# Moving the order of work at three seams of an adaLN attention and gMLP kernel: the first products, the step from attention to the MLP, and the ends of the mixing blocks

## The chip, the core and the metric

The kernel runs on one core of one Trainium2 chip. A core has five engines that run beside each other and wait for one another through semaphores: TensorE (PE in the profile; its weight loads are listed apart as PEld), VectorE (DVE), ScalarE (ACT), GpSimd (POOL) and SyncE (SP), which here only issues DMAs. Each engine works through its own instructions in the order in which the program lists them, so an instruction that waits also holds everything behind it on its engine. Matmul results land in PSUM, which holds 8 banks of 128 x 512 floats here: a ring of seven shared by nearly everything, and one bank of its own.

The metric is the time of one execution on the device in microseconds (us); lower is better. Times of several executions are compared by their median.

## The reference

One block of a network on x of 2048 rows and 448 columns. A conditioning vector c gives six modulation vectors; attention with 16 heads of width 28 comes first, then a gated MLP that mixes along the sequence.

```python
mod = (_silu(c) @ w_mod).reshape(c.shape[0], 6, 1, -1)
sa, ca, ga, sb, cb, gb = ...
h = _layernorm(x) * (1 + ca) + sa
x = x + ga * _A_ref(h, A_wqkv, A_wo)
h = _layernorm(x) * (1 + cb) + sb
x = x + gb * _B_ref(h, B_w_in, B_w_sp, B_b_sp, B_w_out)

# _A_ref: q, k, v = h @ wqkv; p = softmax(q k^T * 28**-0.5); out = (p v) @ wo
# _B_ref: z = gelu(h @ w_in); z1, z2 = halves of z; z2 = layernorm(z2)
#         g = w_sp @ z2 + b_sp;  out = (z1 * g) @ w_out
```

The halves z1 and z2 have 896 columns each, and w_sp is 2048 x 2048.

## The kernel before, in words

Wherever an operand of a large product must keep its precision, it is split into a high part in the PE's fast float format and a low part that is the rest (`sub`, line 71), and the product is summed from three partial products. For an inner width of 448 this gives eleven matmuls per output tile, listed in `STEPS`; the last two of them, `STEPS_Z`, use only slot 6 of the left operand. A "V tile" below is one output of `v_tiles` (128 rows of V, eleven matmuls at line 256, copied out by DVE at line 258), and a "QK unit" is one call of `qk_unit` (128 channels of Q or K for 512 rows, eleven matmuls at line 265, copied and split by ACT and POOL, and written to scratch memory in DRAM by SP).

The stages, in the order of the program:

1. **The first products.** SP loads x in four groups of 512 rows (`load_x`), the modulation weights (`load_mod`, line 152) and wqkv (`load_w`, lines 165, 74, 75). DVE takes the layernorm statistics (`ln_stats`), sums the modulation products (`mod_acc`, lines 199 and 201), and normalises (`ln_norm`, line 238). `mod_col` turns the modulation sums into per-channel columns with PE (line 207) and DVE (line 211). `ln_transpose` transposes a group with PE (line 104) and applies the columns and the split with ACT, DVE and POOL (lines 111 to 122); its result is hT[g]. The loop over g (line 316) then does, for each group, its V tiles, the transposes of the next group, the statistics of the one after, and the QK units of channels 0 and 3 of the same group; before the first QK unit, the four parts of the QK weights are split by `weight_part` (line 353), the low parts by DVE and POOL in turn. All PSUM tiles of this stage come from the seven ring banks in turn, so the n-th tile waits until the reader of the tile seven before it is done.
2. **Attention.** Twenty further QK units are run with the first row-maximum products of head 0 between their matmuls (`m_first`, lines 535 to 548), in an order that needs only the first 1536 rows of q and k at first. Then a hand-written order (line 550) interleaves row-maximum products (line 388, reduced by DVE at line 393), score products (419), exponentials on ACT (423) and the products with V (434). Small per-head steps sit at numbered slots (`at`, `events`), DMAs among them. The result lands in OT, in `heapD`.
3. **The step to the MLP** (from line 666). The last head's sums are inverted (line 680), and its rows are scattered into OT by eight DMAs (line 471), half from SP and half from ACT. `win_load` loads the first half of w_in (lines 652, 74, 75) and `win_prep` splits it (lines 82 and 71). The output projection of 16 row tiles (`wo_mm`, line 599) runs for seven "held" tiles without `STEPS_Z`, then waits for `o_split(3, ...)`, the split of slot 6 (lines 486 to 488; the low parts by DVE and POOL in turn), and finishes them. `wo_add` adds x (line 619), `h2_stats` and `h2_norm` (line 638) do the second layernorm, `h2_group` the transposes, with all low parts on POOL.
4. **z1** (line 717) and **z2** (line 779), the two halves of the gelu product.
5. **Mixing.** For each of four blocks of 512 output rows (tb) and 16 key tiles (st) of w_sp, seven channel tiles (f) are summed into seven PSUM banks with three matmuls each (lines 825 to 827). A w_sp tile is loaded by SP (760), split by ACT (762) and DVE (71); there are two buffers for the raw tile and four for the split ones. The last `nj` key tiles of a block are run channel by channel, so that `gate` can start on a finished channel while PE sums the next: DVE adds and multiplies (lines 842 and 843), ACT and POOL split the result into uT. From the second block on, the output product of the block before (`y_part`, lines 865 to 871) is spread between the key tiles.

Most tiles of the large buffers are views into `heapD`, `heapA` and `heapB`. The lines that the change touches, and those that are named in the prediction:

Of the kernel before, what the change touches and what calls it, by code (L numbers as in the profile page):

```python
# [20 lines left out]
NG = 4  # L21
# [12 lines left out]
def tile_adaln_mha_gmlp(ctx, tc, x, wqkv, wo, w_in, w_spT, b_sp, w_out, cT, w_mod, out):  # L34
# [26 lines left out]
    heapD = dpool.tile([128, 24 * 896], F32R, name="heapD")  # L61
# [6 lines left out]
    wqk = hview(heapD, 14336, 8, 896)  # L68
# [8 lines left out]
    def weight_part(dst, i, raw, hi_eng, lo_eng, zero=True):  # L77

        n = raw.shape[-1]
        h = dst[:, i if i < 3 else 6, :n]  # L80
        if hi_eng is act:
            act.activation(h, raw, AF.Copy)
        else:
            hi_eng.tensor_copy(h, raw)
        if i < 3:
            sub(lo_eng, dst[:, 3 + i, :n], raw, h)
        else:
            sub(lo_eng, dst[0:64, 7, :n], raw[0:64], h[0:64])
            if zero:
                pool.memset(dst[64:128, 7, :n].bitcast(F32), 0.0)  # L90
# [6 lines left out]
    def ln_transpose(xns, full_pool, dsts, scol, bcol, engs, los=(pool,) * 4, mid=None, after=None):  # L97

        tps = []
        for c in range(4):  # L100
            tp = ring.tile([128, 512], F32, name="tp", tag="s")
# [46 lines left out]

    def load_mod(pair, eng):
# [23 lines left out]
    load_mod(0, sp)  # L173
# [3 lines left out]
    pool.memset(wqk[64:128, 7, :].bitcast(F32), 0.0)  # L177
# [8 lines left out]
    wu = ring.tile([128, 512], F32, name="wu", tag="s")  # L186
# [16 lines left out]
    def mod_col(*parts):  # L203
        pc = ring.tile([128, 512], F32, name="pc", tag="s")
        for i, (nm, acc, plus1) in enumerate(parts):
            for c, r, e in ((0, 0, 128), (1, 0, 128), (2, 0, 128), (3, 0, 64), (3, 64, 128)):
                pe.matmul(
                    pc[r:e, 4 * i + c : 4 * i + c + 1], acc[:, c * 128 : c * 128 + e - r], ones[:112, 0:1], start=True, stop=True
                )
        for i, (nm, acc, plus1) in enumerate(parts):  # L210
            dve.tensor_scalar(out=cols[nm], in0=pc[:, 4 * i : 4 * i + 4], scalar1=plus1, scalar2=None, op0=ALU.add)

    def mod_bc(nm, acc):
        pc = ring.tile([128, 512], F32, name="pc", tag="s")
# [18 lines left out]
    def ln_norm(g):  # L233
# [13 lines left out]
        for xn in res:  # L247
            pool.tensor_copy(xn[:, D:], xn[:, 384:D])
        return res

    def v_tiles(*kts):
        pvs = [ring.tile([128, 512], F32, name="pv", tag="s") for _ in kts]
# [7 lines left out]
    def qk_unit(m, g, mid=None):  # L260
        pq = ring.tile([128, 512], F32, name="pq", tag="s")
# [33 lines left out]
    def wv_rest(c):  # L295
        if c == 2:
            wv_hi(1)
# [4 lines left out]

    def mod_first():
        pe_fill(4)
        mod_col(("ca", accs[0][:, 1, :], 1.0), ("sa", accs[0][:, 0, :], 0.0))
# [6 lines left out]
    for i in range(4):  # L312
# [3 lines left out]
    for g in range(NG):  # L316
# [4 lines left out]
        if g == 3:  # L321
            early.close()
            stk = att.enter_context(tc.tile_pool(name="stk", bufs=1))
            kq = {}
            for i, (nm, pad) in enumerate((("k0", 64), ("q0", 0), ("q2", 16), ("k2", 0), ("q1", 8), ("k1", 8))):
                if pad:
                    stk.tile([128, pad], F32, name=f"pad{i}")
                kq[nm] = stk.tile([128, S], F32R, name=f"{nm[0]}st{nm[1]}")
            kst, qst = ([kq[f"{n}{i}"] for i in range(3)] for n in "kq")
# [11 lines left out]
            load_head(0, 0, 1536)  # L341
            for m in (0, 3):
                qk_unit(m, g)
            load_head(0, 1536, S)
# [6 lines left out]
        if g == 0:  # L351
            for i in range(4):
                weight_part(wqk, i, raws.pop(("qk", i)), act, (dve, pool)[i % 2], False)
# [5 lines left out]
        if g > 0:  # L359
            v_tiles(4 * g + 2)  # L360
        else:
            pool.memset(V[:, :, :, DH:32], 1.0)
        v_tiles(4 * g + 3)
        if g == 2:
            mod_bc("ga", accs[1][:, 0, :])
            mod_col(("sb", accs[1][:, 1, :], 0.0))
        if g < 3:
            for m in (0, 3):
                qk_unit(m, g)
        if g in (1, 2):  # L370
            for k in range(4):
                mod_acc(g, k)
    mod_col(("cb", accs[2][:, 0, :], 1.0))
# [11 lines left out]
    def m_mm(j, kb):  # L385
        h, t = divmod(j, NT)
        mt = ring.tile([128, 512], F32, name="mt", tag="s")
# [13 lines left out]
    def m_fin(h):  # L401
        mx = mxs.pop(h)
        tp = ring.tile([128, 512], F32, name="mtp", tag="s")
# [538 lines left out]
```

## Time and profile before

| | us |
|---|---|
| median of 3 executions | 1465.11 (1464.35 to 1467.84) |
| the profiled execution, its own time | 1466.46 |
| its span, first to last instruction | 1464.7 |

The profile is that of one execution. Its span is 1.8 us shorter than its own time; a duration from it is set against the span, and a forecast that is made as a difference is added to the median. "Busy" counts the time in which an engine executes; matmuls are pipelined, and their ends are modelled. A row of a timeline gives start, length, engine, line, operation, output and inputs, how many instructions are merged into it, and in brackets how long the engine had been idle before it and what ended that idle time. A row of the waits gives who waited for whom, the total in us, how many times, and the longest. A row of the windows gives, for one stretch of the span, its length, each engine's busy time with the number of instructions, the clock that was granted to TensorE (1.00 is full), the busy share of the DMA engines, and GB/s.

### The profile page before, as it was taken

What the parts mean: (1) busy time and instruction counts of PE and PEld (TensorE: products, weight loads), DVE (VectorE), ACT (ScalarE), POOL (GpSimd) and SP (SyncE); (2) the same over time, 40 slices, a digit from 0 to 9 for tenths busy, and PEclk for the clock granted to TensorE, in tenths of its full rate; (3) what the DMA queues carried; (4) which work ended last, traced back from release to release, by engine and by line L of the source; (5) the groups of instructions that cost most, each with busy time, mean ns of one, the idle gap of its engine ahead of it and who ended that gap; (6) DMA issues with size and microseconds to landing.
All of it is one profiled execution on the core that took longest, in us unless ns stands there. A gap on an engine that the chain in (4) does not pass through costs nothing.

```text
span 1464.7 us, 19637 instructions
## 1 busy us (share of the span) xinstructions
PE 1436.5 (98%) x7314; PEld 1015.3 (69%) x7314; DVE 884.6 (60%) x1440; ACT 733.1 (50%) x1390; POOL 302.0 (21%) x273
## 2 busy tenths in 40 slices
PE   5899999999999999999999999999999999999999
PEld 5787755555555555555555555888988888888887
DVE  6557888888888888888888832921552411413114
ACT  3523577677677767767776786442432211211111
POOL 6734200000002011001000021520763400302002
PEclk9999999999999999999999999999999999999999
DMA  7554401221022211221012004442002321313223
GB/s 220 146 163 151 145 9 46 52 49 43 15 52 53 53 39 40 53 51 41 21 47 52 11 19 139 151 149 101 8 14 99 119 77 67 113 64 106 84 69 107
DMA packets 56133, 111.24 MB, mean 76 GB/s; under 512 B 11901, under 2 KB 22781, under 8 KB 53517
## 3 DMA queue, kind: packets, MB, share of 16 engines
q1 hardware_dynamic: 55868, 109.76, 25.1%
q8 instruction: 57, 0.93, 0.3%
q10 hardware_dynamic: 168, 0.23, 0.1%
q14 instruction: 40, 0.32, 0.1%
HBM read 75.89 MB, written 29.48 MB: 72 GB/s over the span
## 4 chain that ended last, share of the span: by engine, by line
PE 92%; DVE 2%; POOL 2%; DMA 2%; issue 1%; ACT 0%; SPq 0%; ACTq 0%; DVEq 0%; POOLq 0%
PE st_ps L419 18%; PE mt L388 16%; PE o_ps L434 16%; PE acc L825 7%; PE acc L827 7%; PE acc L826 7%; PE z_ps L779 5%; PE z_ps L717 5%; PE pq L265 4%; PE y_ps L866 2%; PE y_ps L865 2%; PE y_ps L867 2%; PE pv L256 1%; PE tp L104 1%; POOL heapD L71 1%
## 5 line engine op out<-in xcount | busy, mean ns | idle before, releaser
L393 DVE TENSOR_REDUCE pm<-mt 128x1 f32<-128x512 f32 x1024 | 632.0, 681 | 121.8 <-PE mt L388 121.4
L423 ACT ACTIVATE P<-st_ps 128x512 f32<-128x512 f32 x1024 | 514.2, 618 | 154.3 <-PE st_ps L419 153.9
L419 PE MATMUL st_ps<-qst,kst 86*128 86x512 f32 x1024 | 409.8, 411 | 0.0
L388 PE MATMUL mt<-kst,qst 84*128 84x512 f32 x1024 | 406.6, 397 | 0.3 <-DVE pm L393 0.3
L419 PEld LDWEIGHTS st_ps<-qst,kst 86*128 86x128 f32 x1024 | 193.1, 189 | 144.8 <-issue 82.2
L434 PE MATMUL o_ps<-P,V 128*32 128x512 f32 x2048 | 247.5, 598 | 0.0
L388 PEld LDWEIGHTS mt<-kst,qst 84*128 84x128 f32 x1024 | 194.8, 190 | 38.3 <-DVE pm L393 0.7
L71 DVE TENSOR_TENSOR wsp_l<-raw_sp,wsp_h 128x512 fp32r<-128x512 f32 x64 | 53.7, 841 | 185.7 <-ACT wsp_h L762 185.7
L762 ACT ACTIVATE wsp_h<-raw_sp 128x512 fp32r<-128x512 f32 x64 | 40.3, 631 | 229.1 <-DMA raw_sp<-in_w_spT_dram 187.3
L434 PEld LDWEIGHTS o_ps<-P,V 128*32 128x32 f32 x2048 | 54.1, 109 | 123.5 <-issue 116.6
L71 POOL TENSOR_TENSOR heapD<-u,heapD 128x512 fp32r<-128x512 f32 x27 | 44.7, 1692 | 254.0 <-ACT heapD L844 170.2
L460 POOL TENSOR_TENSOR osb<-osb,rb 128x512 f32<-128x512 f32 x15 | 19.2, 1281 | 349.6 <-DMA rb<-r_scr 192.0
L265 PE MATMUL pq<-heapD 128*128 128x512 f32 x308 | 85.8, 396 | 2.9 <-DVE heapD L71 2.9
L825 PE MATMUL acc<-wsp_h,heapD 128*128 128x512 f32 x224 | 87.6, 391 | 0.6 <-DVE u L842 0.6
L827 PE MATMUL acc<-wsp_h,heapD 128*128 128x512 f32 x224 | 87.3, 390 | 0.0
L826 PE MATMUL acc<-wsp_l,heapD 128*128 128x512 f32 x224 | 87.2, 389 | 0.0
L265 PEld LDWEIGHTS pq<-heapD 128*128 128x128 f32 x308 | 58.0, 189 | 16.4 <-DVE heapD L71 3.4
L71 POOL TENSOR_TENSOR nl<-nf,nh 16x128 fp32r<-16x128 f32 x16 | 7.2, 453 | 285.5 <-issue 152.3
L267 ACT ACTIVATE qf<-pq 128x512 f32<-128x512 f32 x28 | 16.7, 597 | 70.1 <-PE pq L265 70.1
L870 DVE TENSOR_TENSOR x2t<-x2t,y_ps 128x448 f32<-128x448 f32 x12 | 7.5, 622 | 72.9 <-PE y_ps L867 72.9
L825 PEld LDWEIGHTS acc<-wsp_h,heapD 128*128 128x128 f32 x224 | 42.1, 188 | 9.7 <-DVE u L842 1.4
L71 POOL TENSOR_TENSOR ql<-qf,qh 128x512 fp32r<-128x512 f32 x28 | 36.4, 1304 | 59.7 <-ACT qh L269 47.2
(150 smaller groups left out, 1693.3 us busy)
## 6 DMA issues: line engine op xcount, KB each, us to landing
raw_sp<-in_w_spT_dram SPq DMA_DIRECT2D x64, 256.0 KB
kst<-qk_scr SPq DMA_DIRECT2D x45, 224.0 KB
qst<-qk_scr SPq DMA_DIRECT2D x45, 224.0 KB
qk_scr<-qh SPq DMA_DIRECT2D x28, 256.0 KB
qk_scr<-ql SPq DMA_DIRECT2D x28, 256.0 KB
z_scr<-z1t SPq DMA_DIRECT2D x28, 256.0 KB
z<-z_scr SPq DMA_DIRECT2D x28, 256.0 KB
wm<-in_w_mod_dram SPq DMA_DIRECT2D x12, 392.0 KB
```

Source lines behind the costliest of these rows:

```text
L71: eng.tensor_tensor(out=dst, in0=a, in1=hi.bitcast(F32), op=ALU.subtract)
L265: pe.matmul(pq, wqk[:, b, m * 128 : (m + 1) * 128], hT[g][:, a, :], start=j == 0, stop=j == NST - 1)
L388: pe.matmul(mt, qst[h % 3][0:84, t * 128 : (t + 1) * 128], kst[h % 3][0:84, kb * 512 : (kb + 1) * 512], start=True, stop=True)
L393: dve.tensor_reduce(out=pms[h][:, t, kb : kb + 1], in_=mt, axis=AX.X, op=ALU.max)
L419: pe.matmul(st, kst[h % 3][0:86, kt * 128 : (kt + 1) * 128], qst[h % 3][0:86, qb * 512 : (qb + 1) * 512], start=True, stop=True)
L423: act.activation(p, st, AF.Exp, scale=SCALE)
L434: pe.matmul(otile[h][32 * qb : 32 * qb + 32, :], V[:, kt, h, :], ptiles.pop((u, qb)), start=kt == 0, stop=kt == NT - 1)
L717: pe.matmul(ps_t, w1[:, b, f * 128 : (f + 1) * 128], h2T[g][:, a, :], start=j == 0, stop=j == NST - 1)
L779: pe.matmul(ps_t[:, :D], h2T[g][:, a, tt * 128 : (tt + 1) * 128], w2[:, b, hf * D : (hf + 1) * D], start=j == 0, stop=j == NST - 1)
L825: pe.matmul(acc[f], z2[st][:, 0, fs], hi, start=st == 0, stop=False)
L826: pe.matmul(acc[f], z2[st][:, 0, fs], lo, start=False, stop=False)
L827: pe.matmul(acc[f], z2[st][:, 1, fs], hi, start=False, stop=st == NT - 1)
```

## The change

It is one diff with edits in each of the stages.

- **First products.** The four DMAs of the first modulation weights are issued by ACT instead of SP. The 64-column copy at the end of a normalised tile moves from POOL to DVE. `mod_col` can do its columns in two halves; the first call does channels 0 and 2, then 1 and 3, and four warm-up matmuls ahead of it go. In the loop, the QK units of a group come one pass later: group 0 is done in pass 1, group 1 in pass 2, and groups 2 and 3 in pass 3, where all four stand ahead of the V tiles of group 3. Pass 0 does V tiles 0 to 2, then the transposes of group 1, then V tile 3, and then the split of the QK weights, with all four low parts on DVE. The first part of head 0 that is loaded back ends at row 1024 instead of 1536, and `first` is ordered to match. The buffers of q and k lose their padding and take another order.
- **w_in during the attention.** The last 4 x 896 columns of `heapD` become a buffer of their own, `heapF`; once the QK weights are done with, it holds the first half of w_in, which is loaded at slots 180 to 204 of the attention. `Halves` joins two buffers into one view.
- **The step to the MLP.** All four groups of x are loaded ahead of the last head's scatter; all four parts of w_in are split at the start of the stage. The scatter is dealt five to SP and three to ACT. Eight tiles are held instead of seven, the eighth in the bank beside the ring. The four low parts of `o_split(3, ...)` and the low parts of `h2_group` go to DVE, and the output tiles 12 to 15 are placed between the pieces of `h2_group`.
- **Mixing.** Every block ends with three key tiles by channel (before: two, and three in the last block). Ahead of the gates of a block, the split of one w_sp tile of the next block is listed instead of two; of the second one only the load is issued, and its split stands behind the gates.

```diff
-    heapD = dpool.tile([128, 24 * 896], F32R, name="heapD")
+    heapD = dpool.tile([128, 20 * 896], F32R, name="heapD")
+    heapF = dpool.tile([128, 4 * 896], F32R, name="heapF", tag="heapF")
...
+    wqk = Halves(4, hview(heapD, 14336, 4, 896), hview(heapF, 0, 4, 896))
...
-    load_mod(0, sp)
+    load_mod(0, act)
...
-            pool.tensor_copy(xn[:, D:], xn[:, 384:D])
+            dve.tensor_copy(xn[:, D:], xn[:, 384:D])
...
     def mod_first():
-        pe_fill(4)
-        mod_col(("ca", accs[0][:, 1, :], 1.0), ("sa", accs[0][:, 0, :], 0.0))
+        parts = ("ca", accs[0][:, 1, :], 1.0), ("sa", accs[0][:, 0, :], 0.0)
+        mod_col(parts, (0, 2))()
+        rest.append(mod_col(parts, (1, 3)))
         pe_fill(10)
...
-            load_head(0, 0, 1536)
-            for m in (0, 3):
-                qk_unit(m, g)
-            load_head(0, 1536, S)
+            load_head(0, 0, 1024)
+            for i in (2, 3):
+                for m in (0, 3):
+                    qk_unit(m, i)
+            load_head(0, 1024, S)
...
-        if g == 0:
-            for i in range(4):
-                weight_part(wqk, i, raws.pop(("qk", i)), act, (dve, pool)[i % 2], False)
         if g + 1 < NG:
             ln_transpose(xns, e1, hT[g + 1], cols["ca"], cols["sa"], (act,) * 4)
         if g + 2 < NG:
             ln_stats(g + 2)
             xns = ln_norm(g + 2)
-        if g > 0:
+        if g == 0:
+            pool.memset(V[:, :, :, DH:32], 1.0)
+            v_tiles(3)
+            for i in (0, 2, 1, 3):
+                weight_part(wqk, i, raws.pop(("qk", i)), act, dve, False)
+        else:
             v_tiles(4 * g + 2)
-        else:
-            pool.memset(V[:, :, :, DH:32], 1.0)
-        v_tiles(4 * g + 3)
+            v_tiles(4 * g + 3)
...
-        if g < 3:
+        if g in (1, 2):
             for m in (0, 3):
-                qk_unit(m, g)
-        if g in (1, 2):
+                qk_unit(m, g - 1)
             for k in range(4):
                 mod_acc(g, k)
...
-                for (sl, r), eng in zip(dests, (sp, act if h == H - 1 else sp)):
-                    eng.dma_start(
+                for (sl, r), i in zip(dests, (2 * qb, 2 * qb + 1)):
+                    (act if h == H - 1 and i in (1, 3, 6) else sp).dma_start(
...
     for i in range(4):
         at(120 + 8 * i, wo_load, i)
         at(124 + 8 * i, wo_prep, i)
+        at(180 + 8 * i, win_first, i)
...
-    HELD = 7
-    x_load(0)
+    for g in range(4):
+        x_load(g)
     for i in range(4):
-        win_load(0, i)
+        raw_in[0, i] = wraw[0][:, i, :]
+        win_prep(0, i, pool)
     wo_mm(0, STEPS_MAIN)
...
     n_scatter(h)
-    for g in range(1, 4):
-        x_load(g)
-    for i in range(2):
-        win_prep(0, i, pool)
     for t in range(1, HELD):
         wo_mm(t, STEPS_MAIN)
-    for qb in range(4):
-        o_split(3, qb, dve if qb % 2 == 0 else pool)
-    for i in range(2, 4):
-        win_prep(0, i, pool)
-    for t in range(HELD):
+    o_split(3, 0, dve)
+    o_split(3, 1, dve)
+    for t in range(4):
         wo_mm(t, STEPS_Z)
         wo_add(t)
+    o_split(3, 2, dve)
+    for t in range(4, 8):
+        wo_mm(t, STEPS_Z)
+        wo_add(t)
+    o_split(3, 3, dve)
     h2_stats(0)
-    wo_tile(7)
     h2_stats(1)
     h2_norm(0)
...
-    for t in (8, 9, 10):
+    for t in range(8, 12):
         wo_tile(t)
     h2_norm(1)
-    wo_tile(11)
-    h2_group(0)
+    wo_mm(12, STEPS)
+    wo_add(12)
+    h2_group(0, lambda c: wo_tile(13) if c == 2 else None)
+    wo_tile(14)
+    h2_group(1, lambda c: wo_tile(15) if c == 2 else None)
     h2_stats(2)
-    wo_tile(12)
-    wo_tile(13)
     h2_norm(2)
-    h2_group(1)
-    wo_tile(14)
-    wo_tile(15)
     h2_stats(3)
...
-            if g == 0 and f == 0:
+            if g == 0 and f == 3:
+                h2_group(2)
                 h2_norm(3)
-            if g == 0 and f in (1, 5):
-                h2_group(2 + f // 5)
+            if g == 1 and f == 1:
+                h2_group(3)
...
-        nj = 3 if tb == NG - 1 else 2
+        nj = 3
...
-        while nl < len(seq) and nl < (tb + 1) * NT + 2:
+        if nl < len(seq):
             wsp_load(nl)
             nl += 1
+            wsp_raw(nl)
```

`h2_group` hands its low parts to DVE and calls the function it is given after each channel group; `win_first` is the load of one part of w_in into `heapF`, and `wsp_raw` the load of one w_sp tile without its split.

## The prediction

> **What bounds the kernel now.** I read the page's busy times first, then the windows cut at the stages, then TensorE's own waits.
>
> ```profile
> PE 1436.5 (98%) x7314; PEld 1015.3 (69%) x7314; DVE 884.6 (60%) x1440; ACT 733.1 (50%) x1390; POOL 302.0 (21%) x273
> ```
> ```profile
> 0.00:96.00 96.00, 76.58 (x399) 66.12 (x400) 53.95 (x94) 36.13 (x54) 60.97 (x63) 0.98 0.60 172
> 165.00:896.00 731.00, 730.97 (x4042) 415.07 (x4041) 582.44 (x979) 530.17 (x1073) 62.58 (x69) 1.00 0.17 41
> 896.00:941.00 45.00, 40.80 (x209) 36.32 (x209) 32.97 (x59) 16.96 (x25) 22.88 (x19) 1.00 0.61 205
> 1086.00:1465.00 379.00, 374.46 (x1683) 315.31 (x1681) 103.26 (x140) 63.09 (x100) 70.70 (x49) 1.00 0.27 88
> ```
>
> TensorE idles 1464.7 - 1436.5 = 28.2 us: 19.4 in the first products, 4.2 in the step to the MLP, 4.5 in the mixing, nothing in the attention. The change removes almost no matmul, so it can only win idle time, and three seams hold it:
>
> ```profile
> PE tp L104 <- DVE xn L238: 12.8, 1, 12.8
> PE pv L256 <- DVE V L258: 3.0, 1, 3.0
> PE pq L265 <- DVE heapD L71: 2.9, 1, 2.9
> PE wo_ps L599 <- POOL heapD L71: 1.7, 1, 1.7
> PE tp L104 <- DVE x L638: 1.5, 1, 1.5
> PE wo_ps L599 <- ACT zt L486: 0.9, 1, 0.9
> PE acc L825 <- DVE u L842: 0.6, 1, 0.6
> ```
>
> **The start.** DVE paces the time to the first V matmul:
>
> ```profile
> 8.16 1.15 DVE L225 BATCH_NORM_STATS2 st<-xg 128x6 f32<-128x448 f32 x2 [2.77 <-DMA xg<-in_x_dram]
> ...
> 11.16 1.15 DVE L201 SCALAR_TENSOR_TENSOR acc<-wm,silu,acc 112x896 f32<-112x896 f32 x1 [0.93 <-DMA wm<-in_w_mod_dram]
> 12.23 1.77 DVE L238 TENSOR_SCALAR xn<-xg,mv,rs 128x448 f32<-128x448 f32 x4
> 13.92 2.36 DVE L201 SCALAR_TENSOR_TENSOR acc<-wm,silu,acc 112x896 f32<-112x896 f32 x2
> ...
> 19.94 0.81 DVE L113 TENSOR_SCALAR hfull<-tp,col_ca,col_sa 128x512 f32<-128x512 f32 x1
> ```
> ```profile
> 0.00:10.00 10.00, 0.00 (x0) 0.00 (x0) 3.69 (x14) 1.49 (x2) 2.17 (x9) 1.00 0.76 214
> 910.00:920.00 10.00, 7.46 (x36) 6.61 (x36) 8.96 (x19) 5.23 (x8) 8.91 (x6) 1.00 0.93 319
> ```
>
> The last x tile lands at 8.16, the second modulation weight only at 11.16. Issued by ACT, the weights (1.6 MB by shape) start with x (0.9 MB) instead of behind it. They wait less, but x now shares the DMA engines, and DVE lists all statistics first. At 214 GB/s, 1.8 MB (equal shares) have moved by 8.4 us; x landed some 2.6 us after its own 0.9 MB could have moved, so I expect it near 11.2. From there: two statistics 1.15, aggregation 0.4, two sums 1.8, normalising 1.8, the four moved copies 0.4 (64 of 448 columns: between 0.06 and the 0.44 of a whole tile each; 0.1 taken, as the width is nearer), two sums 2.4, half of the columns 1.2: 20.4 against 19.94. I take **+0.7**, since the second half of the columns and the ten warm-up matmuls still stand ahead of the V tiles. Bounds: -2.5 (x lands at 8.16 as before) and +2 (x last of all).
>
> The Trainium skill, page "DMA: Bandwidth & Descriptors", section "Issuing engines are not separate DMA queues", says that DMAs of all issuing engines interleave on the same 16 DMA engines and that another issuer saves only issue time. By it the move to ACT brings x later, the upper half of these bounds; no stretch of this trace has ACT and SP load large tiles together.
>
> **The loop over groups.** Two waits are cured: the QK units no longer wait for the split weights (2.9), and V tile 11 no longer waits behind the modulation sums (3.0).
>
> ```profile
> 32.24 6.02 DVE L71 TENSOR_TENSOR heapD<-raw,heapD 128x896 fp32r<-128x896 f32 x2
> 38.19 2.19 DVE L225 BATCH_NORM_STATS2 st<-xg 128x6 f32<-128x448 f32 x4
> ...
> 43.83 1.78 DVE L238 TENSOR_SCALAR xn<-xg,mv,rs 128x448 f32<-128x448 f32 x4 [3.16 <-POOL rs L95]
> ```
> ```profile
> 48.91 4.73 PE L256 MATMUL pv<-wv,heapD 128*128 128x448 f32 x22
> ```
> ```profile
> 68.00:70.00 2.00, 0.00 (x0) 0.00 (x0) 2.00 (x3) 1.35 (x2) 2.00 (x2) 1.00 1.04 278
> 72.00:73.00 1.00, 1.00 (x4) 0.88 (x3) 0.00 (x0) 0.00 (x0) 0.04 (x1) 0.50 0.59 168
> ```
>
> The 3.0 us wait is followed by half clock (0.50), some 1.6 us more. What is late next? On DVE the list is now: normalise group 2, copy V3, four low parts of the QK weights, copy V4. V tile 7 takes V4's bank, seven tiles later. Normalising waits for POOL's rstd, which stands behind the low parts of hT[1]; it ended at 43.8 with two QK low parts ahead of it on POOL, which now go (3.0 each in DVE's row, so 0 to 6 us; I take 3.8): 40.0. Then 1.8 + 0.4 + 0.6 (a V copy, an estimate from a 448-column add of 0.56 below) = 42.8. The low parts: two took 6.02 beside POOL, so four take at most 12; scaled from 0.69 per 512 columns (a row below) at least 4.8; POOL is idle for the first half, so I take 6.2, the nearer end. V4's copy ends at 49.6. TensorE gets there at: V4 waits for hT[1], whose last low part ends just ahead of that rstd, until about 38.9, V5 2.4 (4.73 for two), transposes 1.9 and a 0.6 wait, V6 2.4, so 45.7 at unchanged start. A **new wait of 3.9 us**, with half clock behind it as before. Sum: -2.9 - 3.0 + 1.0 (V4) + 0.6 + 3.9 = **-0.4**; bounds -3.5 (fast low parts, no half clock) and +2.
>
> **Attention.** The w_in loads (1.8 MB) go where the DMA engines are 17% busy: nothing. Without that cover a head's rows come 0.5 us later per issue. The order by 1024 rows needs its second part only after four QK units of main loop: nothing. The removed padding: nothing that the trace shows.
>
> **The step to the MLP.** TensorE's list without a wait, from the held tiles on:
>
> ```profile
> 898.16 11.72 PE L599 MATMUL wo_ps<-heapD 128*128 128x448 f32 x54
> ```
> ```profile
> 941.29 5.16 PE L717 MATMUL z_ps<-heapB,heapA 128*128 128x512 f32 x22
> ```
> ```profile
> 923.26 3.19 DVE L638 TENSOR_SCALAR x<-x,mv,rs 128x64 f32<-128x64 f32 x8 [0.89 <-POOL rs L95]
> 926.37 1.68 DVE L619 TENSOR_TENSOR x<-x,wo_ps 128x448 f32<-128x448 f32 x3
> 927.96 7.34 DVE L638 TENSOR_SCALAR x<-x,mv,rs 128x64 f32<-128x64 f32 x8
> ```
>
> 167 matmuls at 0.21 and two transposes of 1.9 end at 937.2; z1 began at 941.29, so 4 us are there to win. The first held wait: 63 matmuls last until 911.8. The scatter now stands behind 3.7 MB of x instead of 1.8 MB of w_in; at 319 GB/s x is in at about 909, ACT and DVE split the first quarter by 911.5: no wait, though barely. DVE then sets the pace. Eight normalising steps took 3.19 alone and 7.34 beside POOL's low parts; with these on DVE (0.69 each) POOL is quiet. DVE's list from 912.3: 16 adds of 0.56, three statistics of 2.5, three normalisings of 3.2, two splits and eight low parts of 0.7, and about 4 of waits for ACT and POOL: 37, so group 2 is normalised at 949.4. TensorE reaches its transposes after four z1 units of 2.6, at 947.5, and waits 1.9. Net **-2.0**; bounds -3.8 (no wait) and +0.5 (the scatter late).
>
> **The ends of the mixing blocks.** By channel, three key tiles are nine matmuls at 0.225 (379 us over 1683), 2.0 us per channel, 14.2 for the seven. The second and third end have SP held by the output of the block before:
>
> ```profile
> 1335.42 0.63 DVE x2t L870
> ...
> 1337.96 4.81 DMA raw_sp<-in_w_spT_dram
> ```
> ```profile
> 1343.54 0.69 DVE L71 TENSOR_TENSOR wsp_l<-raw_sp,wsp_h 128x512 fp32r<-128x512 f32 x1 [2.65 <-ACT wsp_h L762]
> 1344.15 0.68 DVE L842 TENSOR_TENSOR u<-acc,bt 128x512 f32<-128x512 f32 x1
> ```
> ```profile
> 1353.64 0.68 DVE L842 TENSOR_TENSOR u<-acc,bt 128x512 f32<-128x512 f32 x1
> ```
> ```profile
> 1355.50 0.63 ACT L844 ACTIVATE heapD<-u 128x512 fp32r<-128x512 f32 x1 [1.06 <-DVE u L843]
> ```
>
> Take T = 1335.2, the end of the last full key tile in the new order. The first raw tile of the next block is issued behind the output and two z1 loads, at T + 2.3, and lands 4.4 to 4.8 later; split by ACT and DVE, it lets the gates begin at T + 8.1, as DVE's order puts them behind it (before: T + 8.9 for the second tile). Last add 9.5 later, at T + 17.6; ACT's copy 1.9 after it ends at T + 20.1; only then come the high part of the second tile (0.63) and its low part (0.69), ready at T + 21.5. TensorE ends the seven channels at T + 14.2, needs 21 matmuls (4.7) for the first tile, and wants the second's high part at T + 18.9 and its low part at T + 19.1. So it waits 2.3 us at two ends. At the first end no output holds SP, the gates keep up with 2.0 per channel, and the split comes in time. The 0.6 wait of before goes. Net **+4.0**; bounds -0.6 (the tile in time) and +6.
>
> **Sum**: 0.7 - 0.4 - 2.0 + 4.0 = +2.3. Against the profiled 1466.46 that is 1468.8; against the median, 1465.1 + 2.3 = **1467.4**.
>
> **The rivals.**
> - *The shared waits don't appear*: x lands as early as before (-2.5), the low parts run fast (-1.5 in the loop), and the second tile comes in time (-0.6), with -2.0 at the step: -6.6, 1458.5. For it: x is only 0.9 MB, and ACT is busy 63 us of 379 in the mixing. Against it: DVE's fixed order in both places.
> - *Half clock after the new mixing waits* (the slower side). Place: the first key tiles of the last two blocks. Price: 3.4 us at half clock lose 1.7 each, as after 70; +2.3 + 3.4 = +5.7, 1470.8. It decides if 2.3 us in one stretch of 3.4 count as idle: with 3.0 idle it did, after the 2.9 wait it did not, so the alignment decides. The Trainium skill, page "TensorE: Matmul & The Clock Gate", section "Part 1: The HAM clock gate", gives halving after at least one idle window of about 3.4 us. By it this rival never happens; the trace already halved after a shorter wait.
> - *The step wins nothing*: x ahead of the scatter makes the first split late by 2 us, +4.3, 1469.4. Against it: the 319 GB/s.
>
> **How the numbers follow.** The forecast 0.45; the first rival 0.20; half clock 0.25; the lost step 0.10, half of it beyond +4.4. A difference of 0.3%, 4.4 us, is about what a measurement of this kernel can tell from no change. Faster 0.20, same 0.50, slower 0.30. The range reaches from the first rival to half clock with x at its late bound and the mixing at its upper one: 1459 to 1474.
>
> **What would show it.** Right: DVE's first statistics end after 10 us; a TensorE wait on the copy of V near 46 to 50; z1 beginning near 937 with a wait on normalised x near 948; two waits of TensorE at line 825's successors on the split of w_sp, none at the first block's end. Wrong: the gates beginning under 5 us after the last full key tile, a first transpose before 12.8, or any change of pace in the attention.

## The result: 14 us slower, and the profile after

The changed kernel takes 1478.66 us in the median (1478.30 to 1479.34) against 1464.73 for the kernel before beside it; the ratio is 1.0091, with a 95% interval of 1.0074 to 1.0109. The prediction was 1467.4 with a range of 1459 to 1474: too low by 11.3, and outside the range. The profiled execution took 1479.34, with a span of 1477.5 us, 12.8 more than before.

The page's first two parts, of the changed kernel:

```profile
span 1477.5 us, 19602 instructions
...
PE 1442.0 (98%) x7306; PEld 1016.7 (69%) x7306; DVE 892.1 (60%) x1478; ACT 731.6 (50%) x1390; POOL 267.9 (18%) x237
```

TensorE idles 35.5 us instead of 28.2, and is busy 5.5 us longer on nearly the same matmuls. Most of the 5.5 is clock: between its first full clock and the end of its work, TensorE was granted half clock for 13.7 us of this profile, against 3.4 us before, and half of its busy time in them is 6.2 against 1.7 us, 4.5 more (an estimate). The windows, cut near the stages at rounded times (columns: length, then busy time and instructions of PE, PEld, DVE, ACT and POOL, granted clock, DMA share, GB/s):

```profile
0.00:26.70 26.70, 8.52 (x57) 7.67 (x57) 14.10 (x33) 4.52 (x7) 7.95 (x13) 1.00 0.66 198
26.70:104.30 77.60, 71.71 (x340) 60.14 (x339) 42.42 (x82) 31.26 (x47) 43.79 (x33) 0.93 0.49 147
104.30:177.00 72.70, 71.52 (x302) 56.13 (x302) 55.39 (x82) 23.82 (x40) 26.64 (x21) 1.00 0.46 156
177.00:904.00 727.00, 726.99 (x4032) 412.59 (x4030) 581.24 (x976) 529.67 (x1071) 61.10 (x68) 1.00 0.18 44
904.00:945.00 41.00, 40.57 (x210) 36.48 (x210) 29.01 (x56) 14.75 (x22) 12.39 (x9) 1.00 0.51 180
945.00:1092.00 147.00, 145.73 (x695) 127.58 (x694) 62.84 (x114) 64.76 (x104) 47.01 (x46) 1.00 0.21 73
1092.00:1477.00 385.00, 376.91 (x1682) 316.14 (x1680) 107.14 (x139) 62.85 (x100) 69.04 (x49) 1.00 0.28 87
```

The stages are, in order: the start, up to the first V tile; the loop over groups, up to the first row-maximum product; the first row maxima, up to the first score product; the rest of the attention; the step to the MLP, up to z1; z1 and z2; the mixing. Cut exactly at the first matmul of each, they take 26.7, 77.7, 72.6, 727.2, 41.2, 146.7 and 385.4 us here, and 21.8, 74.9, 70.4, 728.6, 45.5, 145.0 and 378.4 us in the kernel before. So the start lost 4.9, the loop 2.8, the first row maxima 2.2; the rest of the attention won 1.4, the step to the MLP 4.3; z1 and z2 lost 1.8 and the mixing 7.0. The sum is 12.9, the whole difference of the spans. TensorE's waits (us in total, times, longest) name them:

```profile
PE tp L116 <- DVE xn L267: 18.5, 3, 17.4
PE pv L285 <- DVE V L287: 3.6, 1, 3.6
PE acc L867 <- ACT wsp_h L804: 2.7, 2, 1.4
PE acc L868 <- DVE wsp_l L83: 2.3, 2, 1.1
PE pv L285 <- POOL heapD L83: 1.5, 2, 0.9
PE tp L116 <- DVE x L675: 1.3, 3, 0.4
```

Against the list of before: the first wait is 4.6 longer (17.4 instead of 12.8), the wait of a V tile on a copy is still there, the wait of the QK units is gone, the waits of the output projection have nearly gone, and the two waits of the mixing are new.

### The profile page after: what moved, and what is told of

It is laid out like the page before. It is cut to its first block, busy times and chain, and to the rows that moved or that the text cites. A ratio compares the mean times of both kernels' runs of the same rounds, so it can differ in the third digit from the quotient of the medians.

```text
span 1477.5 us, 19602 instructions
## 1 busy us (share of the span) xinstructions
PE 1442.0 (98%) x7306; PEld 1016.7 (69%) x7306; DVE 892.1 (60%) x1478; ACT 731.6 (50%) x1390; POOL 267.9 (18%) x237
## 4 chain that ended last, share of the span: by engine, by line
PE 89%; DVE 4%; DMA 3%; issue 2%; POOL 1%; ACT 1%; SPq 0%; DVEq 0%; ACTq 0%; POOLq 0%
PE st_ps L448 18%; PE mt L417 16%; PE o_ps L463 16%; PE acc L868 6%; PE acc L869 6%; PE acc L867 6%; PE z_ps L821 5%; PE pq L294 4%; PE z_ps L752 4%; PE y_ps L908 2%; PE y_ps L907 2%; PE y_ps L909 2%; DMA xg<-in_x_dram 1%; PE pv L285 1%; PE wo_ps L636 1%
## 5 line engine op out<-in xcount | busy, mean ns | idle before, releaser
L83 POOL TENSOR_TENSOR heapF<-u,heapD 128x512 fp32r<-128x512 f32 x27 | 43.3, 1632 | 262.1 <-ACT heapD L886 262.1
L294 PE MATMUL pq<-heapD 128*128 128x512 f32 x196 | 62.8, 397 | 0.5 <-DVE pm L422 0.5
L867 PEld LDWEIGHTS acc<-wsp_h,heapD 128*128 128x128 f32 x224 | 42.3, 189 | 12.5 <-ACT wsp_h L804 3.6
L868 PEld LDWEIGHTS acc<-wsp_l,heapD 128*128 128x128 f32 x224 | 42.5, 190 | 11.4 <-DVE wsp_l L83 3.1
L869 PEld LDWEIGHTS acc<-wsp_h,heapD 128*128 128x128 f32 x224 | 42.5, 190 | 9.0
```

The costliest lines, as they stand in the source:

```text
L83: eng.tensor_tensor(out=dst, in0=a, in1=hi.bitcast(F32), op=ALU.subtract)
L294: pe.matmul(pq, wqk[:, b, m * 128 : (m + 1) * 128], hT[g][:, a, :], start=j == 0, stop=j == NST - 1)
L867: pe.matmul(acc[f], z2[st][:, 0, fs], hi, start=st == 0, stop=False)
L868: pe.matmul(acc[f], z2[st][:, 0, fs], lo, start=False, stop=False)
L869: pe.matmul(acc[f], z2[st][:, 1, fs], hi, start=False, stop=st == NT - 1)
```

## The experiments

All runs change the changed kernel, except where the kernel before is named. A ratio is to the kernel before, run on the same chip; the kernel before took 1464.7 to 1468.7 on the chips used, so ratios are compared, not times.

**1. The weights issued by SP again.**

```python
-    load_mod(0, act)
+    load_mod(0, sp)
```

> The changed kernel with one line undone: the first modulation weights are issued by SP behind x again, not by ACT. Theory A (the weights took DMA time from x, whose last tile landed at 11.89 instead of 8.14 us, and everything to the first V tile moved with it): the last x tile is back near 8.2, the first V matmul comes some 3 us earlier than in the changed kernel (26.68), near 23.5, and the time falls by 2 to 4 us to about 1475.5. It does not come back to 21.8, since the normalising is still slowed beside GpSimd. Rival B (x is late for another reason, for instance the order of its own rows, and the late normalising is due to the moved copies alone): the first V matmul stays within 1 us of 26.7 and the time within 1 us of 1478.7.

Measured: 1473.40 us, ratio 1.0043 (1.0026 to 1.0059). DVE's normalising, POOL's next instruction and TensorE's first V tiles, first of the changed kernel (its x landed at 11.89), then of this one (8.28):

```profile
16.05 3.40 DVE L267 TENSOR_SCALAR xn<-xg,mv,rs 128x448 f32<-128x448 f32 x4 [0.94 <-POOL rs L107]
15.99 2.36 POOL L83 TENSOR_TENSOR wv<-raw,wv 128x448 fp32r<-128x448 f32 x2
26.68 7.42 PE L285 MATMUL pv<-wv,heapD 128*128 128x448 f32 x33
```
```profile
12.69 1.78 DVE L267 TENSOR_SCALAR xn<-xg,mv,rs 128x448 f32<-128x448 f32 x4
16.04 3.15 POOL L83 TENSOR_TENSOR wv<-raw,wv 128x448 fp32r<-128x448 f32 x2 [4.45 <-ACT wv L311]
21.59 7.42 PE L285 MATMUL pv<-wv,heapD 128*128 128x448 f32 x33
```

The first V tile comes 5.1 us earlier, more than Theory A allowed, and even 0.2 before the kernel before; the time falls by 5.3 us between the medians, 7.0 by the ratios, where 2 to 4 were expected. The issue by ACT did two things: x landed 3.6 us later, and the V weights, queued behind fewer DMAs on SP, landed earlier (12.6 instead of 15.4), so that GpSimd split them just while DVE normalised. Of the four normalising steps of the changed kernel, the two that meet a split took 1.31 and 1.32 us, the other two 0.50 each; here all four take 0.51. Theory A said that the slow normalising would stay; it went, since the two no longer meet.

**2. The same line in the kernel before.**

```python
-    load_mod(0, sp)
+    load_mod(0, act)
```

> The kernel before with one line of the change: ScalarE issues the first modulation weights instead of SP. Theory A (x shares DMA time with the weights; the slow normalising came in only because GpSimd, freed of the copies of the moved columns, splits the V weights at that moment): the last x tile lands near 11.9 us, the four normalising steps take 1.8 us together as before, the first V matmul comes 3 to 4 us later than 21.8, and the time is 2.5 to 4.5 us above the kernel before. Rival B (the issue by ScalarE alone makes the normalising slow too): the steps take over 3 us and the time rises by 5 us. Rival C (the loss is not from this line): within 1 us of the kernel before.

Measured: 1468.98, ratio 1.0022 (1.0008 to 1.0036), about 3.2 us slower. x landed at 11.57, the normalising is not slowed, and the first V tile comes at 25.16, 3.35 later than before:

```profile
15.73 1.78 DVE L238 TENSOR_SCALAR xn<-xg,mv,rs 128x448 f32<-128x448 f32 x4 [0.94 <-POOL rs L95]
```

Theory A holds. In the kernel before, POOL still has the moved copies to do, which wait for the normalising and hold the split of the V weights back. So of the 4.9 us at the start, some 3.3 are the later landing of x. The other 1.6 are as much as the normalising lost beside POOL's split, which in run 2 stands behind the copies. No run puts the copies alone back, so this second part is read from the rows.

**3. The banks in turn from the first row maximum on.** `bank` names one of seven tags; up to there it repeats the banks of the changed kernel.

```python
+    turn = [1, 0, 6, 5, 4, 3, 2, 3, 0, 5, 1, 2, ...]
     def bank(name):
-        return ring.tile([128, 512], F32, name=name, tag="s")
+        if not turn:
+            turn.extend([4, 3, 2, 6, 5, 1, 0])
+        return ring.tile([128, 512], F32, name=name, tag=f"s{turn.pop(0)}", bufs=1)
...
```

> The changed kernel with the PSUM banks named: up to the first row-maximum product every tile gets the bank that it had in the changed kernel, and from there on the seven ring banks strictly in turn. Theory A (the 2.2 us lost at 132 to 140 us come from the banks: six row-maximum tiles in a row were given the bank of the tile just before and waited for its reduction): the stretch from the first row-maximum product to the first score product shrinks from 72.6 to about 70.4 us, no wait of line 417 on the reduction longer than 0.4 us is left, and the time falls by about 2 us to 1476.5. Rival B (the second half of the rows of q and k, loaded in a new order, comes late, or VectorE is the bound there): the same six waits remain and the time stays within 0.7 us of 1478.7.

Measured: 1478.95, ratio 1.0083 (1.0068 to 1.0098). Here is the chain of work of the changed kernel at the place in question (start, us, what). It is a strict alternation, a row maximum and its reduction, with only the QK matmuls that fit between:

```profile
132.08 0.70 DVE pm L422
...
132.82 0.51 PE mt L417
...
133.36 0.70 DVE pm L422
...
134.10 0.51 PE mt L417
```

As read from the built program, these tiles have one and the same bank, and each waits until DVE has reduced the tile just before it. In the changed kernel the first row maximum comes at 104.34 and the first score product at 176.97, 72.6 us apart; here their rows are (first start behind the durations):

```profile
L422 PE MATMUL mt<-kst,qst x1024: 389/395/501, 104.8 to 862.5; 84*128 84x512 f32 x171
L453 PE MATMUL st_ps<-qst,kst x1024: 387/399/505, 175.6 to 902.0; 86*128 86x512 f32 x171
```

The 72.6 became 70.8 us and the six waits are gone: Theory A for the stage, with 1.8 us of the 2.2. In their place one wait of 0.7 us on ACT (line 422 on line 301) appears. But the time did not follow: from the first to the last score product it takes 726.4 instead of 724.1 us (726.3 in run 11, the other run with banks in turn there; 723.5 to 725.5 in all others). Banks in turn were worse in the attention, so this run does not show the 2 us in the time.

**4. The mixing ends of before.**

```python
-        nj = 3
+        nj = 3 if tb == NG - 1 else 2
...
-        if nl < len(seq):
+        while nl < len(seq) and nl < (tb + 1) * NT + 2:
             wsp_load(nl)
             nl += 1
-            wsp_raw(nl)
```

> The changed kernel with the ends of the mixing blocks of the kernel before: two key tiles by channel in the first three blocks, and both first tiles of the next block split ahead of the gates. Theory A (the split of the second tile behind the gates costs 2.5 us at two ends, and the second of these waits brings half clock for 3.4 us, 1.7 more): the two waits of 1.4 and 1.1 us at lines 867 and 868 go, the span from the first accumulation to the end of it falls by 6 to 7 us, and the time is about 1472. Rival B (the waits are late landings of w_sp, which the old order shares): at least 3 us of the waits remain and the time is above 1475.

Measured: 1472.23, ratio 1.0037 (1.0024 to 1.0050). The waits on w_sp are gone, and from the first to the last accumulation it takes 357.9 us instead of 364.4 (before: 357.4), and no half clock is left in the mixing. Theory A.

**5. The split of the second tile inside the last gate.**

```python
-    def gate(tb, f, lo_eng):
+    def gate(tb, f, lo_eng, mid=None):
...
         dve.tensor_tensor(out=u, in0=acc[f], in1=bt[tb], op=ALU.add)
+        if mid is not None:
+            wsp_load(mid)
...
+            mid = nl if f == 6 and nl < len(seq) else None
...
```

> The changed kernel with three key tiles by channel, but the split of the second w_sp tile placed between the add and the product of the last gate, not behind them (its buffer comes free only when the last channel is done, so no earlier place is open). Theory A (the two waits are the place of the split in VectorE's and ScalarE's order): each end waits 0.3 to 1.3 us instead of 2.5, the half clock of the third end goes, and the time falls by 3.5 to 5.5 us to about 1474. Rival B (w_sp lands late or the split's own time decides): the waits stay above 2 us each and the time above 1477.

Measured: 1472.07, ratio 1.0043 (1.0027 to 1.0058). In the changed kernel, DVE, ACT and PE at the second block's end read:

```profile
1268.07 1.60 DVE L83 TENSOR_TENSOR wsp_l<-raw_sp,wsp_h 128x512 fp32r<-128x512 f32 x1 [1.30 <-ACT wsp_h L804]
```
```profile
1266.89 0.63 ACT L886 ACTIVATE heapD<-u 128x512 fp32r<-128x512 f32 x1 [1.07 <-DVE u L885]
1267.43 0.61 ACT L804 ACTIVATE wsp_h<-raw_sp 128x512 fp32r<-128x512 f32 x1
```
```profile
1268.09 0.51 PE L867 MATMUL acc<-wsp_h,heapD 128*128 128x512 f32 x1 [1.36 <-ACT wsp_h L804]
1269.73 0.50 PE L868 MATMUL acc<-wsp_l,heapD 128*128 128x512 f32 x1 [1.13 <-DVE wsp_l L83]
```

The raw tile had landed at 1254.8; the high part starts only when ACT has done the last gate's copy, and TensorE waits for it, then for the low part. With the split one instruction earlier, the row of this run is

```profile
PE acc L868 <- DVE wsp_l L83: 2.0, 2, 1.1
```

and the span of the accumulations is 359.5 instead of 364.4 us, again without half clock. Theory A: it is the place in the order, not the landing. The time fell by 6.6 us between the medians, 7.0 by the ratios, more than the 3.5 to 5.5 expected.

**6. The sums behind the copies.**

```python
...
             v_tiles(4 * g + 1)
+        if g == 2:
+            for k in range(4):
+                mod_acc(1, k)
+            load_mod(2, sp)
...
-            for k in range(4):
+            for k in range(4 if g == 2 else 0):
                 mod_acc(g, k)
```

> The changed kernel with the sums of the second pair of modulation vectors moved on VectorE behind the copies of V tiles 8 and 9 (and the third pair's weights issued there). Theory A (V tile 11 waits 3.6 us because its bank is that of V tile 8, whose copy stands behind these four sums): the wait goes, with it the 6.8 us of half clock that follow it (3.4 lost), so the first row-maximum product comes 5 to 7 us earlier than 104.3 and the time is 1472 to 1474. Rival B (the copy is late because normalising group 3, slowed beside GpSimd, holds VectorE): the wait shrinks by less than 1.5 us, the half clock stays, and the time is above 1476.

Measured: 1480.69, ratio 1.0091 (1.0076 to 1.0106). No gain, and neither theory as stated. The place in the changed kernel, DVE and then PE:

```profile
59.89 3.74 DVE L267 TENSOR_SCALAR xn<-xg,mv,rs 128x448 f32<-128x448 f32 x4 [3.43 <-POOL rs L107]
...
65.73 5.34 DVE L216 SCALAR_TENSOR_TENSOR acc<-wm,silu,acc 112x896 f32<-112x896 f32 x3
71.00 1.67 DVE L287 COPY V<-pv 128x448 f32<-128x448 f32 x3
```
```profile
65.57 2.49 PE L285 MATMUL pv<-wv,heapD 128*128 128x448 f32 x11
71.66 4.47 PE L285 MATMUL pv<-wv,heapD 128*128 128x448 f32 x11 [3.61 <-DVE V L287]
```

With the sums later the wait of V tile 11 on its bank is gone, but the products that use these sums stand next in TensorE's list, and wait just as long:

```profile
PE pc L244 <- DVE acc L216: 3.7, 1, 3.7
```

**7. The sums and their products later.** As in run 6, and:

```python
-        if g == 2:
-            mod_bc("ga", accs[1][:, 0, :])
-            mod_col((("sb", accs[1][:, 1, :], 0.0),))()
         if g in (1, 2):
             for m in (0, 3):
                 qk_unit(m, g - 1)
+            if g == 2:
+                mod_bc("ga", accs[1][:, 0, :])
+                mod_col((("sb", accs[1][:, 1, :], 0.0),))()
...
```

> The changed kernel as in the run with the sums later, and the two products that read these sums (the row of ga, the column of sb) also moved, behind the QK units of that turn, so that TensorE meets them some 5 us later. In the run with the sums later alone V tile 11 no longer waited, but TensorE waited 3.7 us on these products instead. Theory A (the sums were the last thing late at this place): no wait over 1 us is left between 60 and 90 us, the half clock there goes, the first row-maximum product comes 4.5 to 6.5 us earlier than 104.3, and the time is 1472 to 1475. Rival B (VectorE has no room at all there, so that any order gives the wait to another): a wait of 2 us or more appears at a third place and the time stays above 1477.

Measured: 1474.25, ratio 1.0055 (1.0037 to 1.0073). The first row maximum comes at 98.57 instead of 104.34, with no wait of TensorE and no half clock between 60 and 90: Theory A.

**8. Three parts undone**: runs 1, 4 and 7 together.

> The changed kernel with SP issuing the weights, the sums and their products later, and the mixing ends of the kernel before; the step to the MLP and the rest of the loop stay changed. If the three losses add (5 at the start, 5 in the loop, 6.5 in the mixing, some half clock counted twice): 1478.7 less 14 to 17, that is 1462 to 1465, 1 to 4 us under the kernel before, and the gain is that of the step to the MLP (2.5) less the six bank waits (2.2) and what the loop wins. If the losses hide each other: above 1468.

Measured: 1461.43, ratio 0.9969 (0.9958 to 0.9981), 4.5 us faster than the kernel before, a little more than the 1 to 4 expected: the losses add, and do not hide each other. TensorE's four longest waits, none of them on a copy of V, a modulation sum or a split of w_sp:

```profile
PE tp L116 <- DVE xn L267: 13.1, 1, 13.1
PE pv L285 <- POOL heapD L83: 1.5, 2, 0.9
PE tp L116 <- DVE x L679: 0.9, 2, 0.4
PE acc L871 <- DVE u L888: 0.7, 1, 0.7
```

**9. The same with named banks.** Its `bank` reads the tag from a written list: the banks of run 8, except that the 100 tiles between the first row maximum and the first score product go in turn.

```python
+    turn = iter(TURN)
     def bank(name):
-        return ring.tile([128, 512], F32, name=name, tag="s")
+        return ring.tile([128, 512], F32, name=name, tag="s" + next(turn), bufs=1)
...
```

> The kernel with three parts undone, and its banks named: up to the first row-maximum product and from the first score product on each tile has the bank that it had there, and only the 100 tiles between them go in turn. Theory A (the six bank waits cost 2 us; the 2.3 us that the attention lost when all its banks went in turn came from its own banks, not from naming them): the stretch from the first row-maximum to the first score product is 70.4 to 71.0 us instead of 72.6, the attention keeps its 705 us (between the 17th and the 2001st product with V), and the time is 1.5 to 2.5 us under the kernel with three parts undone, about 1459.3. Rival B (the matmuls lost there come back later in the attention, which VectorE or ScalarE paces): the time stays within 0.7 us of that kernel.

Measured: 1460.35 against 1468.73 for the kernel before on that chip, ratio 0.9944 (0.9931 to 0.9958). First row maximum and first score product:

```profile
L447 PE MATMUL mt<-kst,qst x1024: 389/395/502, 91.9 to 847.3; 84*128 84x512 f32 x171
L478 PE MATMUL st_ps<-qst,kst x1024: 387/395/504, 162.7 to 886.8; 86*128 86x512 f32 x171
```

70.8 us, and the attention keeps its 724.1 from the first to the last score product: Theory A for both stretches. In the time the size is less sure: the median is 1.1 us under that of run 8, by the ratios it is 3.7, and the two intervals just touch.

**10. The padding back**, the six q and k tiles placed as before.

> The changed kernel with the order and the padding of the six q and k tiles as before. The stretch from the 17th to the 2001st product with V took 706.46 us before and 705.07 to 705.57 in four kernels without the padding. Theory A (where q and k lie in memory gives the 1.0 to 1.4 us): 706.3 or more here. Rival B (it is another part of the change, the loads of w_in or the banks that fall to the tiles): 705.6 or less.

```python
-            kq = [[stk.tile([128, S], F32R, name=f"{n}st{i}") for n in "kq"] for i in range(3)]
+            kq = {}
+            for i, (nm, pad) in enumerate((("k0", 64), ("q0", 0), ("q2", 16), ("k2", 0), ("q1", 8), ("k1", 8))):
+                if pad:
+                    stk.tile([128, pad], F32, name=f"pad{i}")
...
```

Measured, one execution: 1480.70 us; the stretch takes 705.88 us, between the two theories. Run 2, with the padding throughout, has 705.74, and runs 5 and 7, without it, 704.50 and 704.47. These single executions spread as widely as the 1.4 us in question. Inconclusive; yet the three traces with the padding (705.7 to 706.5) all lie above the eight without it and without banks in turn (704.5 to 705.6), so where q and k lie is not ruled out.

**11. All banks in turn from the first tile on.** As run 3, but:

```python
-    turn = [1, 0, 6, 5, 4, 3, 2, 3, 0, 5, 1, 2, ...]
+    turn = []
...
-            turn.extend([4, 3, 2, 6, 5, 1, 0])
+            turn.extend(range(7))
...
```

> The changed kernel with all ring banks strictly in turn from the first tile on, as the prediction took it. Then V tile 7 has the bank of V tile 4, whose copy ended at 54.07 in the changed kernel behind four low parts, while TensorE came to V tile 7 near 51.8. Theory A (the prediction's new wait was only avoided because the allocator gave V tile 7 another bank): TensorE waits 1.5 to 2.5 us on the copy of V near 52, and 2.2 us less among the first row-maximum products. Rival B (the copies are early enough in any case): no wait over 0.5 us near 52.

Measured, one execution: 1477.42 us. The wait on the copy of V appears:

```profile
54.05 2.51 PE L290 MATMUL pv<-wv,heapD 128*128 128x448 f32 x11 [1.59 <-DVE V L292]
```

Theory A, with 1.59 us; the stretch of the first row maxima shrank by 1.8. The wait of V tile 11 became 1.35, without half clock, and the first row maximum comes at 101.4, so up to there this order was no worse than the allocator's.

## Why the prediction was wrong, step by step

**The start, +0.7 taken, +4.9 measured: the step that failed most.** Its first half was right: x lands at 11.89 (11.2 forecast), since the weights share the DMA engines. The Trainium skill, page "DMA: Bandwidth & Descriptors", section "Issuing engines are not separate DMA queues", had it so, and runs 1 and 2 agree: 3.6 and 3.4 us of landing for one line. What failed is the path behind it. "DVE paces the time to the first V matmul" was misread: in the kernel before, DVE sat idle for 3.4 us ahead of the columns, waiting for TensorE, and the changed kernel has the same wait, though shorter:

```profile
19.67 0.16 DVE L211 TENSOR_SCALAR col_ca<-pc 128x4 f32<-128x4 f32 x1 [3.38 <-PE pc L207]
```
```profile
23.58 0.16 DVE L232 TENSOR_SCALAR col_ca<-pc 128x2 f32<-128x2 f32 x1 [1.48 <-PE pc L225]
```

TensorE first does sixteen transposes, which begin with the first normalised tile, then the products for the columns. The first V tile follows the first transpose by 9.3 us here and by 9.0 before, so a late x moves it by nearly its whole delay. On DVE's own list, "two sums 2.4, half of the columns 1.2: 20.4" became 23.84. Of these 3.4 us, x is 0.7, and 0.8 is a wait for POOL, which computes the reciprocal of the deviation (`rs`), and which the sum left out (before, DVE was waiting for the weights at that time). "Normalising 1.8" became 3.40, with the moved copies 1.5 more than forecast, because POOL was free to split weights beside it; the columns were 0.5 later.

The Trainium skill, page "SBUF — State Buffer", section "Who interferes with whom", says that a DVE `tensor_scalar` in a two-port mode and a GpSimd operation hold the same ports in turn, the other fully blocked; the trace agrees, with two steps of 1.3 us that each end 0.25 us after a split on POOL, and 1.6 us lost in all beside 2.4 us of POOL. I had counted POOL's relief as free, although my own rows of the step to the MLP showed normalising at 7.34 us beside POOL and 3.19 alone.

**The loop, -0.4 taken, +2.8 measured.** The QK wait did go. "V tile 11 no longer waits behind the modulation sums (3.0)" failed: nothing in the change takes the four sums from ahead of the copy of V tile 8, whose bank V tile 11 has; 3.0 became 3.6, and the half clock behind it is 6.8 us long instead of 3.4. Runs 6 and 7 show that it takes two moves, sums and products, to be rid of it, worth 5.8 us at the first row maximum. The new wait of 3.9 us at V tile 7 did not come: the allocator gave that tile a bank of the transposes. So the banks of this stage are not taken in turn, as the description of the kernel and the prediction took it. With banks really in turn (run 11) the wait is 1.59 us: right in place, too large by 2.3. (The terms of that estimate add up to 46.2 for TensorE's arrival, not 45.7, which makes 0.5 of it.) The waits of V tile 4 on hT[1], 1.0 forecast, are 0.64 and 0.91, with half clock behind them.

In sum TensorE's idle time in the loop fell by 0.7 us, near the forecast of 0.4, but by luck: one wait that stayed stands against one that never came. The loss is in TensorE's busy time, 71.8 instead of 68.3 us. Some 2.8 of these 3.5 us are half clock (an estimate: half of the busy time in the stretches at half clock, 4.5 us here and 1.7 before), which the sum held at what it was before.

**The attention, 0 taken, +0.8 measured**: +2.2 and -1.4. Of the 2.2, 1.8 are the six bank waits, shown by runs 3, 9 and 11; the 0.4 left over in those runs may be their new wait on ACT, which no run isolates. No view of before shows the allocator's choice for a program not yet built; the trace of before has one such step, a 0.3 us wait of line 388 on line 393, which I passed over. Where the 1.4 come from stays open (run 10); they may be no more than the spread of single executions.

**The step to the MLP, -2.0 taken, -2.5 measured: right.** From the first held tile to z1 it takes 41.2 instead of 45.5 us, 4.3 won where 4.0 were forecast, and the transposes of group 2 give 1.8 back where 1.9 were: they take 3.6 instead of 1.8 us, with three waits of 0.4 on DVE's normalising.

**The ends of the mixing, +4.0 taken, +7.0 measured: mechanism right, price too low.** At the first end nothing waits; at the others TensorE waits 1.36 + 1.13 and 1.38 + 1.14 us, 2.5 in sum where 2.3 were forecast. The parts are not as forecast: the high part came earlier than thought (a wait of 1.8 by the prediction's own terms), the low part later, since it took 1.60 us beside POOL, not 0.69. TensorE's idle time in the stage grew by 4.4 us, which is these waits less the 0.6 that went. Its busy time grew by 2.6, from 374.2 to 376.8. Of this 1.7 is half clock behind the last wait, as the rival said, at one of its two places. Most of the other 0.9 may be the four restarts, an estimate: a matmul's row ends 0.39 us after its start and the next matmul starts after 0.23, so each wait in the list begins some 0.17 us late. Run 5 shows that it is the place of the split in the order.

**The sum.** The premise that the change "can only win idle time" left the clock out: by the estimates above, 4.5 of the 12.9 us are half clock. The rival with half clock came nearest in the mixing and gave 1470.8; no rival held a late start together with an uncured loop. The bounds of the start (+2), the loop (+2) and the mixing (+6) were all exceeded; the first two came from DVE's list, without TensorE's and POOL's.

## What to carry to other kernels

When a step is moved off an engine, ask what that engine now does at that moment, and beside whom: here the copies taken from POOL let its weight split run into the normalising. When a wait is to be cured, name the instruction that ends it and check that the change moves that one, and then what stands next in the waiting engine's list. Where an allocator deals out buffers, read which buffer a tile gets in the built program; a rotation is an assumption.

## What the runs showed of the hardware

Half clock starts and ends on a fixed grid. Three stretches of the changed kernel, windows on that grid:

```profile
39.90:43.35 3.45, 1.91 (x9) 1.24 (x8) 1.70 (x4) 3.42 (x6) 2.18 (x2) 1.00 1.08 278
43.35:46.77 3.42, 3.17 (x9) 2.30 (x7) 1.88 (x7) 0.77 (x1) 2.17 (x3) 0.50 0.81 224
67.25:70.66 3.41, 0.81 (x4) 0.40 (x3) 3.38 (x2) 1.91 (x3) 3.41 (x3) 1.00 0.80 225
70.66:74.07 3.41, 2.41 (x7) 2.15 (x8) 2.01 (x4) 0.90 (x2) 2.84 (x2) 0.50 0.74 217
74.07:77.49 3.42, 3.42 (x10) 2.38 (x8) 0.62 (x1) 0.00 (x0) 0.00 (x0) 0.50 0.01 5
1364.31:1367.72 3.41, 1.73 (x6) 1.23 (x7) 2.11 (x2) 1.11 (x2) 1.57 (x2) 1.00 0.40 124
1367.72:1371.14 3.42, 3.42 (x9) 2.65 (x8) 0.87 (x2) 0.72 (x2) 0.00 (x0) 0.50 0.60 204
```

From 43.35 to 1367.72 are 388 steps of 3.4133 us. In these rows a step at full clock with TensorE idle for 1.5 to 2.6 us is followed by a step at half clock; a step already at half clock was sometimes followed by another (here with 1.0 us idle), sometimes not. Over the thirteen traces, every full-clock step with 1.9 us idle or more was followed by half clock, none with less than 1.5, and between these it went both ways (1.81 idle without half clock in the kernel before at 33.8, 1.53 with it in run 1 at 34.7). So two waits of 1.4 and 1.1 us cost 1.7 us more or not, by where the grid falls: at the second end of the mixing they brought no half clock in the changed kernel, and 3.4 us of it in runs 1 and 7. The Trainium skill, page "TensorE: Matmul & The Clock Gate", section "Part 1: The HAM clock gate", gives the free-running window of 3413 ns, which agrees, and halving after at least one idle window; these traces halve after windows in which TensorE was idle for only 1.5 to 3.2 of the 3.41 us.

The start has a second clock effect. In nine traces the first record of full clock came 3.6 to 5.8 us after the first transpose, in runs 3, 5, 8 and 11 only 12.8 to 13.5 us after it. In these four the twenty warm-up matmuls took 4.63 us instead of 2.50. In runs 3, 5 and 11 the first V tile came at 29.6 to 30.1, against 26.3 to 27.1 in the changed kernel and runs 4, 6, 7 and 10, though nothing ahead of it differs but the names of banks. What decides this is not shown here. In the traces that runs 1 and 2 compare, the warm-ups took 2.50 each time.
